# Cutting the stores of four wo gradients and the last wq gradient into row pieces in a one-core attention and MLP backward kernel

## The chip, the core and the metric

The kernel runs on one core of a Trainium2 chip. The metric is the device time of one execution in microseconds. Before the change it is 729.2 us, the median of three runs that lie between 728.81 and 729.43. The core has 16 DMA engines, and each transfer between SBUF (the core's on-chip memory, 128 partitions) and HBM is spread over some or all of them by rows of partitions.

## What is computed

The reference runs one decode step of a block and its gradients. With `xn = layernorm(x)`, the output is `x + attention(xn) + mlp(xn)`: 32 heads with a K and a V cache of 8192 x 128 each, and a gated MLP of width 1728. Returned are the output row and the gradients of x, of both caches, of wq and wo, and of the three MLP weights.

```python
q = (x @ wq).reshape(B, Sq, Hq, Dh).transpose(0, 2, 1, 3)
scores = einsum("bhqd,bhkd->bhqk", q, k) * (Dh ** -0.5)
p = softmax(scores); o = einsum("bhqk,bhkd->bhqd", p, v)
A = o.transpose(0, 2, 1, 3).reshape(B, Sq, Hq * Dh) @ wo
out = x + A + B(xn);  grads = vjp(grad_out)
```

As there is one query position, every weight gradient is an outer product of two vectors. The gradients of the caches, 32 heads x 2 x 2 MB, are outer products too, and are as large as the caches that are read.

## The kernel before

A K or V tile of one head is 128 partitions x 8192 elements, 16 KB a partition, 2 MB. Ten slots hold such tiles. A head's K and V are loaded, transposed and multiplied on PE; then the gradients are written over the tiles by DVE (line 466), and the same tiles are stored as the gradients of the caches. All of these loads and stores are issued by SP, in one order (`fifo`, line 105): a tile's store, and then the next load into a slot that has come free. SP waits in that order, for DVE before a store and for the landing of an old store before a load into its slot.

Heads are worked in groups of four (`GH`, `NG` = 8 groups). A group has a wq tile (128 partitions x 5 x 512 elements, five runs of 1 KB a partition) and a wo tile (128 partitions x 4 x 640, four runs of 1280 bytes a partition). Both are 640 KB. There are three buffers of each. Once a group's heads are done, its gradients are written over the tiles while the next group's heads run: `fin_wo` (line 518) at the first head, `fin_wq` (line 524) in five steps over the second and third. After the last step of group g, the weights of group g+3 are loaded by POOL (GpSimd) into the buffers that came free, so POOL waits at line 111 until the old gradient has landed.

The stores of these gradients go through `store_group` (line 505), which has three ways:

- groups 1 to 5, wq: rows 0 to 4 and 5 to 125 by POOL (line 508), the last two rows by SP
- all other stores of groups 0 to 6: all 128 rows in one transfer by POOL (line 512)
- group 7, both gradients: rows 0 to 67 by SP, then 68 to 72 and 73 to 127 by POOL (line 516)

Group 7's gradients are the last large work: after the outer products of head 31, `fin_od`, `fin_pe`, `fin_wo` and `fin_wq` run for it, then a short chain gives the gradient of x, and SP issues the small output rows (lines 850 and 868). The MLP with its gradients runs once, ahead of head 2; POOL stores its gradients. Each of the four engines and SP has its own instruction order; it is the order in which the program is written.

Of the kernel before, what the change touches and what calls it, by code (L numbers as in the profile page):

```python
# [16 lines left out]
P = 128  # L17
# [4 lines left out]
def kernel(  # L22
# [22 lines left out]
    nc = tc.nc  # L45
# [8 lines left out]
    GH = 4  # L54
    NG = H // GH
    GW = GH * DH
# [23 lines left out]
    dwq_v = out_4.rearrange("(ci p) n -> p ci n", p=P)  # L80
    dwo_v = out_5.rearrange("(h p) c -> p h c", p=P)
# [22 lines left out]
    def fifo(out_, in_):  # L104
        nc.sync.dma_start(out_, in_)
# [3 lines left out]
    def load_group(g, eng):  # L109
        wq_g = wpool.tile([P, NC, GW], BF16, name="wq_g", tag="wq_g")  # L110
        eng.dma_start(wq_g[:], wq_v[:, :, g * GW:(g + 1) * GW])
        wo_g = wpool.tile([P, GH, D], BF16, name="wo_g", tag="wo_g")
        eng.dma_start(wo_g[:], wo_v[:, g * GH:(g + 1) * GH, :])
        grp[g] = dict(wq=wq_g, wo=wo_g)
# [387 lines left out]
        for hh in range(GH):  # L502
            out_row(G_["od_bf"][:, hh, 0:1], G_["wo"][:, hh, :])

    def store_group(g, dst, t, split=False):
        if split:
            for lo, hi in ((0, 5), (5, 126)):
                nc.gpsimd.dma_start(dst[lo:hi], t[lo:hi])
            fifo(dst[126:P], t[126:P])
            return  # L510
        if g < NG - 1:
            nc.gpsimd.dma_start(dst, t[:])
            return
        fifo(dst[0:68], t[0:68])
        for lo, hi in ((68, 73), (73, P)):
            nc.gpsimd.dma_start(dst[lo:hi], t[lo:hi])

    def fin_wo(g):
        G_ = grp[g]
        for hh in range(GH):  # L520
            nc.vector.tensor_scalar(G_["wo"][:, hh, :], g_bc[:], G_["od"][:, hh, 0:1], None, ALU.mult)
        store_group(g, dwo_v[:, g * GH:(g + 1) * GH, :], G_["wo"])

    def fin_wq(g, ci):
        G_ = grp[g]
        wq_g, dqb = G_["wq"], G_["dqb"]
        nc.vector.scalar_tensor_tensor(wq_g[:, ci, :], wq_g[:, ci, :], 1.0, dqb, ALU.mult, ALU.mult,  # L527
                                       accum_out=dxa[:, ci, g:g + 1])
        nc.vector.tensor_scalar(wq_g[:, ci, :], dqb, xn_col[:, ci:ci + 1], None, ALU.mult)
        if ci == NC - 1:  # L530
            store_group(g, dwq_v[:, :, g * GW:(g + 1) * GW], wq_g, 1 <= g <= 5)
            grp.pop(g)
            if g + 3 < NG:
                load_group(g + 3, nc.gpsimd)
# [149 lines left out]
    def side_k(h):  # L684
        g, hh = divmod(h, GH)
        if hh == 1 and g > 0:
            fin_wq(g - 1, 0)
        elif hh == 2 and g > 0:
            fin_wq(g - 1, 3)
        elif hh == 3 and g + 1 < NG:  # L690
            prep_do(g + 1, 1)

    def side_m(h):
        g, hh = divmod(h, GH)
        if hh == 0 and g > 0:
            fin_od(g - 1)
        elif hh == 1 and g > 0:
            fin_wq(g - 1, 1)
        elif hh == 2 and g > 0:
            fin_wq(g - 1, 4)  # L700
        elif hh == 3 and g + 1 < NG:
            prep_do(g + 1, 2)
            prep_do(g + 1, 3)

    def side_v(h):
        g, hh = divmod(h, GH)
        if hh == 0 and g > 0:
            fin_wo(g - 1)
        elif hh == 1 and g > 0:
            fin_wq(g - 1, 2)  # L710
        elif hh == 2 and g + 1 < NG:
            prep_new(g + 1)
            prep_do(g + 1, 0)
        elif hh == 3 and g + 1 < NG:
            prep_cm(g + 1, hd[h]["m"][:, 324:324 + 4 * GH])
# [120 lines left out]
    fin_od(NG - 1)  # L836
    fin_pe(NG - 1)
    fin_wo(NG - 1)
    for ci in range(NC):
        fin_wq(NG - 1, ci)  # L840
# [58 lines left out]
```

## Time and profile before

| what | value |
|---|---|
| median of three runs | 729.2 us (728.81 to 729.43) |
| the profiled execution | 730.06 us |
| its span, first to last instruction | 728.3 us |
| PE, DVE, ACT, POOL busy | 600.8, 460.1, 375.7, 35.0 us |
| moved by DMA | 303.53 MB, mean 417 GB/s |
| HBM read, written | 151.34 MB, 151.34 MB |
| DMA issues of wo gradients by POOL | 7 of 640 KB, and 25 and 275 KB for the last |
| DMA issues of wq gradients by POOL | 2 of 640 KB, 5 of 605 KB, 6 of 25 KB, 1 of 275 KB |
| DMA issues of both by SP | 340 KB twice (last group), 10 KB five times |

Each time from the trace is in microseconds from the span's start. The profiled execution's own time is 1.76 us longer than its span, for what lies ahead of the first instruction and after the last. The DMA share of a stretch is the mean over the 16 engines. Queue q1 is that of SP's transfers, q0 that of POOL's, q8 and q14 fetch instructions. The trace also has a record of every packet of a DMA engine: start, duration, bytes and queue.

### The profile page before, as it was taken

How to read it: one execution, taken by the hardware profiler on the slowest of the kernel's cores; microseconds unless marked ns; L12 is line 12 of the kernel's file. 1: busy time of each engine (PE TensorE's matmuls, PEld its weight loads, DVE VectorE, ACT ScalarE, POOL GpSimd, SP SyncE). 2: the span in 40 equal slices, each digit the busy share in tenths (PEclk: the TensorE clock that was granted, in tenths of full speed). 3: DMA queues.
4: the chain of work that ended last, by engine and by line, in shares of the span. 5: the costliest groups of instructions: out<-in, count | busy, mean ns of one | idle time of the engine just before them, and what ended most of it. 6: DMA issues, size and time to landing. Idle time of an engine off the chain costs nothing.

```text
span 728.3 us, 12951 instructions
## 1 busy us (share of the span) xinstructions
PE 600.8 (82%) x5193; PEld 375.6 (52%) x5193; DVE 460.1 (63%) x811; ACT 375.7 (52%) x727; POOL 35.0 (5%) x52
## 2 busy tenths in 40 slices
PE   3989589999999999877986889878896987988840
PEld 2547456665566556544554555445563555644520
DVE  4169646677767886767556746556755665677482
ACT  3640736665666656544554546455562555645410
POOL 0010110000100000000010000000000000000000
PEclk9996799999999999999999989999998999999975
DMA  9999999999999999999999999999999999999996
GB/s 347 398 409 424 427 428 428 413 427 425 418 409 429 427 426 424 423 429 422 425 425 427 431 420 427 421 427 432 410 428 424 428 425 422 429 424 430 429 415 239
DMA packets 28358, 303.53 MB, mean 417 GB/s; under 512 B 3481, under 2 KB 5532, under 8 KB 11658
## 3 DMA queue, kind: packets, MB, share of 16 engines
q1 hardware_dynamic: 22022, 277.14, 90.4%
q0 software_dynamic: 6272, 25.56, 8.8%
q8 instruction: 41, 0.67, 0.4%
q14 instruction: 19, 0.16, 0.1%
q10 hardware_dynamic: 4, 0.00, 0.0%
HBM read 151.34 MB, written 151.34 MB: 416 GB/s over the span
## 4 chain that ended last, share of the span: by engine, by line
DMA 57%; PE 33%; DVE 5%; ACT 2%; issue 1%; SPq 0%; ACTq 0%; DVEq 0%
DMA out_dram<-kv 30%; DMA kv<-in_A_k_cache_dram 18%; PE pT L318 15%; DMA kv<-in_A_v_cache_dram 7%; PE sA L339 4%; PE X L433 3%; PE dA L339 3%; DVE kv L466 2%; PE m L356 2%; DMA wo_g<-in_A_wo_dram 2%; ACT KT L320 1%; PE gu_ps L562 1%; PE dh_ps L573 1%; DVE side L257 0%; PE pT L266 0%
## 5 line engine op out<-in xcount | busy, mean ns | idle before, releaser
L320 ACT COPY KT<-pT 128x512 f32<-128x512 f32 x512 | 287.7, 587 | 230.9 <-PE pT L318 210.3
L318 PE MATMUL pT<-ident_f,kv 128*128 128x128 f32 x2048 | 306.6, 289 | 61.6 <-DMA kv<-in_A_k_cache_dram 29.9
L318 PEld LDWEIGHTS pT<-ident_f,kv 128*128 128x128 f32 x2048 | 236.2, 148 | 155.1 <-issue 59.6
L466 DVE TENSOR_TENSOR kv<-qd,U 128x4096 bf16<-128x4096 bf16 x64 | 146.0, 2283 | 0.0
L466 DVE TENSOR_TENSOR kv<-qd,P 128x4096 bf16<-128x4096 bf16 x64 | 143.5, 2283 | 0.0
L433 PE MATMUL X<-kv,Z 128*32 128x512 bf16 x1024 | 93.5, 402 | 1.8 <-DVE Z L450 1.8
L339 PE MATMUL sA<-KT,qz 128*32 128x512 bf16 x512 | 83.9, 408 | 0.0
L339 PE MATMUL dA<-KT,qz 128*32 128x512 bf16 x512 | 83.3, 404 | 0.0
L416 DVE SCALAR_TENSOR_TENSOR U<-m,P 128x64 bf16<-128x64 f32 x32 | 7.5, 234 | 83.0 <-PE m L356 83.0
L382 DVE TENSOR_REDUCE mrow<-m 128x1 f32<-128x64 f32 x32 | 7.2, 223 | 75.1 <-PE m L356 75.0
L339 PEld LDWEIGHTS <-qz 128*32 128x32 bf16 x1024 | 29.6, 95 | 40.4 <-issue 37.7
L433 PEld LDWEIGHTS <-Z 128*32 128x32 bf16 x1024 | 32.4, 99 | 33.8 <-issue 5.7
L356 PE MATMUL m<-selc,KT 64*128 64x64 f32 x256 | 30.7, 243 | 8.6 <-ACT KT L346 8.6
L356 PEld LDWEIGHTS m<-selc,KT 64*128 64x128 f32 x256 | 21.7, 145 | 30.4 <-ACT KT L346 21.6
L376 ACT CAST qd<-pT 128x256 bf16<-128x256 f32 x32 | 11.9, 372 | 40.3 <-DVE kv L466 28.8
L389 DVE TENSOR_REDUCE negM<-m 128x1 f32<-128x128 f32 x32 | 9.3, 291 | 33.2 <-PE m L386 33.2
L527 DVE SCALAR_TENSOR_TENSOR wq_g<-wq_g,side 128x512 bf16<-128x512 bf16 x40 | 27.3, 682 | 0.0
L257 DVE SCALAR_TENSOR_TENSOR side<-wo_g,g_bc 128x640 bf16<-128x640 bf16 x32 | 26.2, 819 | 1.4 <-DMA wo_g<-in_A_wo_dram 1.1
L448 DVE SCALAR_TENSOR_TENSOR U<-m,P 128x128 bf16<-128x128 f32 x32 | 11.4, 355 | 15.8 <-PE m L446 15.8
L406 DVE RECIPROCAL rZ<-m 128x1 f32<-128x1 f32 x32 | 5.3, 166 | 24.2 <-PE m L400 24.2
L346 ACT COPY KT<-dA 64x512 f32<-64x512 f32 x32 | 18.6, 583 | 2.6 <-PE dA L339 2.6
L346 ACT COPY KT<-sA 64x512 f32<-64x512 f32 x32 | 18.6, 580 | 2.3 <-PE sA L339 2.1
(164 smaller groups left out, 377.4 us busy)
## 6 DMA issues: line engine op xcount, KB each, us to landing
out_dram<-kv SPq DMA_DIRECT2D x64, 2048.0 KB, 30.9
kv<-in_A_k_cache_dram SPq DMA_DIRECT2D x32, 2048.0 KB, 27.9
kv<-in_A_v_cache_dram SPq DMA_DIRECT2D x32, 2048.0 KB, 26.0
wq_g<-in_A_wq_dram POOLq DMA_DIRECT2D x7, 640.0 KB, 13.5
wo_g<-in_A_wo_dram POOLq DMA_DIRECT2D x7, 640.0 KB, 19.6
out_dram<-wo_g POOLq DMA_DIRECT2D x7, 640.0 KB, 15.6
kv<-in_B_w_dram SPq DMA_DIRECT2D x2, 1728.0 KB
out_dram<-kv POOLq DMA_DIRECT2D x2, 1728.0 KB, 23.2
```

The costliest lines, as they stand in the source:

```text
L257: nc.vector.scalar_tensor_tensor(junk[:], G_["wo"][:, hh, :], 1.0, g_bc[:], ALU.mult, ALU.mult, accum_out=G_["do"][:, hh:hh + 1])
L318: nc.tensor.transpose(pT[:, k * P:(k + 1) * P], W3[:, 4 * c + k, :], ident_f[:])
L320: nc.scalar.copy(KT[:].rearrange("p k w -> p (k w)"), pT[:])
L339: nc.tensor.matmul(S_[kind][q:q + QW, :], lhsT=S_["qz"][:, o:o + QW], rhs=KTb[c][:, par, :], start=(c0 == 0 and par == 0), stop=(c0 == NCH ...
L346: nc.scalar.copy(XS[0:QH].rearrange("p k w -> p (k w)"), S_.pop(kind)[0:QH, :])
L356: nc.tensor.matmul(S_["m"][:, b0:b0 + 4 * J].rearrange("p (x c k t) -> p k x c t", x=4, k=4, t=2)[:, k], lhsT=XS[0:QH, k, :], rhs=selc[0:Q ...
L376: nc.scalar.copy(qd[:].rearrange("p a d -> p (a d)"), hd[h].pop("ps_r"))
L389: nc.vector.tensor_reduce(S_["negM"][:], S_["m"][:, 2 * J:2 * J + P], AX.X, ALU.max, negate=True)
L433: nc.tensor.matmul(xg["X"][q:q + QW, :], lhsT=Z[:, o:o + QW], rhs=W[:, N4 * i:N4 * (i + 1)], start=(slot == 0 and i < 4), stop=(slot == NS ...
L448: nc.vector.scalar_tensor_tensor(S_["U2"][:], S_["V"][:, 0:J].unsqueeze(2).to_broadcast([P, J, 2]), S_["m"][:, OC + NS:OC + NS + 1], S_["P ...
L466: nc.vector.tensor_tensor(dst[:, lo * DH:hi * DH].rearrange("p (j a b) -> p j a b", a=DH // 2, b=2), vec.rearrange("p (a b) -> p a b", b=2 ...
L527: nc.vector.scalar_tensor_tensor(wq_g[:, ci, :], wq_g[:, ci, :], 1.0, dqb, ALU.mult, ALU.mult, accum_out=dxa[:, ci, g:g + 1])
```

## The change

`store_group` now takes a list of row counts, and issues one transfer for each: by POOL if the count is positive, by SP if it is negative. For most gradients the pieces are as before. What differs:

- wo of group 0 leaves as 5, 119 and 4 rows, that of group 1 as 5, 51, 4 and 68, those of groups 2 and 3 as 76, 2 and 50, all by POOL, where each was one transfer of 128 rows by POOL
- wq of group 7 leaves as 5, 51 and 72 rows by POOL, where it was 68 rows by SP and 5 and 55 by POOL

So POOL issues ten transfers more and SP one fewer. No instruction of PE, DVE or ACT changes.

```diff
-    def store_group(g, dst, t, split=False):
-        if split:
-            for lo, hi in ((0, 5), (5, 126)):
-                nc.gpsimd.dma_start(dst[lo:hi], t[lo:hi])
-            fifo(dst[126:P], t[126:P])
-            return
-        if g < NG - 1:
-            nc.gpsimd.dma_start(dst, t[:])
-            return
-        fifo(dst[0:68], t[0:68])
-        for lo, hi in ((68, 73), (73, P)):
-            nc.gpsimd.dma_start(dst[lo:hi], t[lo:hi])
+    def store_group(g, dst, t, pieces):
+        lo = 0
+        for n in pieces:
+            eng = nc.gpsimd if n > 0 else nc.sync
+            eng.dma_start(dst[lo:lo + abs(n)], t[lo:lo + abs(n)])
+            lo += abs(n)
+        assert lo == P
+
+    DWO_PIECES = {0: (5, 119, 4), 1: (5, 51, 4, 68), 2: (76, 2, 50), 3: (76, 2, 50), NG - 1: (-68, 5, 55)}
+    DWQ_PIECES = {**{i: (5, 121, -2) for i in range(1, 6)}, NG - 1: (5, 51, 72)}
...
-        store_group(g, dwo_v[:, g * GH:(g + 1) * GH, :], G_["wo"])
+        store_group(g, dwo_v[:, g * GH:(g + 1) * GH, :], G_["wo"], DWO_PIECES.get(g, (P,)))
...
-            store_group(g, dwq_v[:, :, g * GW:(g + 1) * GW], wq_g, 1 <= g <= 5)
+            store_group(g, dwq_v[:, :, g * GW:(g + 1) * GW], wq_g, DWQ_PIECES.get(g, (P,)))
```

## The prediction

> **What bounds the kernel now.** I read the DMA rows first, because a core that moves 303.53 MB in 728.3 us can hardly be bound by anything else. Columns of the queue rows: packets, MB, and the time of their packets as a share of 16 DMA engines.
>
> ```profile
> DMA  9999999999999999999999999999999999999996
> ...
> q1 hardware_dynamic: 22022, 277.14, 90.4%
> q0 software_dynamic: 6272, 25.56, 8.8%
> q8 instruction: 41, 0.67, 0.4%
> q14 instruction: 19, 0.16, 0.1%
> ```
>
> Every slice but the last is full, and the shares add up to 99.7%. The busiest compute engine, PE, has 82%. So the 16 DMA engines are the bound, and what remains to be won is at the end, where they do not stop together. The windows (length, busy times of five engines, clock, DMA share, GB/s) show that:
>
> ```profile
> 716.00:720.00 4.00, 0.37 (x1) 0.09 (x1) 0.41 (x2) 0.00 (x0) 0.00 (x0) 0.50 0.93 331
> 720.00:722.00 2.00, 0.00 (x0) 0.00 (x0) 0.00 (x0) 0.00 (x0) 0.00 (x0) 0.50 0.67 232
> 722.00:724.00 2.00, 0.00 (x0) 0.00 (x0) 0.00 (x0) 0.00 (x0) 0.00 (x0) 0.50 0.39 134
> 724.00:726.00 2.00, 0.00 (x0) 0.00 (x0) 0.00 (x0) 0.00 (x0) 0.00 (x0) 0.50 0.08 33
> 726.00:728.30 2.30, 0.00 (x0) 0.00 (x0) 0.00 (x0) 0.00 (x0) 0.00 (x0) 0.50 0.02 7
> ```
>
> No compute engine works after 720, and a share of 0.08 is little more than one engine in 16 (0.0625). One DMA engine sets the end. The final waits of SP (total us, times, longest) say for what:
>
> ```profile
> SPq L894 <- DMA out_dram<-wq_g: 5.4, 2, 4.6
> SPq L894 <- DMA out_dram<-kv: 1.6, 1, 1.6
> ```
>
> The kv store comes in last; the weight gradients are in before it. They matter because they take that engine's time, not by their own landing.
>
> **Which engine that is.** The records of single packets carry no engine number, but a packet starts 3 to 4 ns before the one ahead of it on its engine ends, so they can be chained into 16 rows. (Where two rows end in the same ns I used that a kv transfer is 8 packets of 16 KB per engine and then one of 4 bytes; ends are therefore sure as a set, and to each single row within a class only probably.) From 10 to 695 us hardly any engine is ever idle, so an engine's end is its own sum of work. The classes, in span time:
>
> - **E0 to E3** end at 721.4 to 724.5. SP's 68-row pieces at the end went to these four engines, 17 rows each. The numbers are names that I give.
> - **E4** ends at 721.8. With E0 to E3 it is in the class that got one row of each 5-row piece. Its 16 KB packets are the slowest (from 138 us on, 13.5 us in all over 611 ns each; the others 2.3 to 9.3).
> - **E5 to E15** got 11 rows of each 121-row piece (each shows thirteen packets of 4096 bytes and one of 3072, that is 55 KB; 55 packets of 3072 bytes in all is 5 groups x 11 engines), and 5 rows of each 55-row piece.
> - **E8 to E15**: eight of these eleven also carry PE's instruction fetches, strictly in turn, 5 each, and one the 41st as well. A fetch takes 0.88 to 1.15 us, and the packet behind one of them took 1.006 us in place of 0.611. The three without fetches, **E5 to E7**, end first, at 718.0 to 718.5. The other seven of the eight end at 720.7 to 724.2; the one with six fetches, which I call E8, ends at 727.0 with a 16 KB kv packet. Its sixth fetch is at 703.0.
>
> The mean end is 722.1, so perfect balance would be worth 4.9 us; the second-last engine ends 2.5 us before E8.
>
> **Where the pieces go.** 121 rows on 11 engines, 55 on 11 and 5 on 5 is "the largest divisor up to 16". The 5-row piece took the same five engines in all groups: each piece continues at the engine behind the last one's, and 5+11 comes back to E0. That the turn follows my numbering inside the eleven (E5 to E7 first, the fetch carriers after them) is assumed; no row shows it. So, rows per engine:
>
> - gradient 0 (5,119,4): E0-4 1, E5-11 17, E12-15 1
> - gradient 1 (5,51,4,68): E0-4 1, E5-7 17, E8-11 1, E12-15 17
> - gradients 2 and 3 (76,2,50), each: E0-3 19, E4-5 1, E6-15 5
> - last wq (5,51,72): E0-4 1, E5-7 17, then 72 over 12 engines: E8-15 and E0-3 6 more
>
> Against 8 rows a gradient before (4 x 8 = 32): E0-3 40, E4 4, E5 36, E6-7 44, E8-15 28. All sets but the last add up to 16, so the order holds.
>
> **The sum for E8.** (1) The wo rows: 4 fewer. A wo row is one packet of 5120 bytes, median 200 ns, shortest 196, less 3.5 overlap: 0.192 us; -0.77 us. (2) The last wq: 5 rows were 25 KB (six packets of 4096 at 159 ns and one of 1024 at 46: 0.975 us); 6 rows are seven and one of 2048 (not in the trace; between those two, I take 0.085): 1.174 us; +0.20. (3) Ten more GpSimd transfers (four become thirteen, two become three). 44 transfers left 775 packets of 4 bytes and 482 of 12 to 16, 6 to 7 ns net each: 11 ns per engine and transfer; +0.11. Sum **-0.46 us**. A row holds up no one else, so nothing more goes with it.
>
> What is late next: E6 and E7, +12 wo rows (2.3) and 17 rows of wq in place of 5 (3.31 - 0.975 = 2.3) and 0.1: 718.3 + 4.8 = 723.1. E5: 721.6. E0-3: +8 wo rows (1.5, partly in their idle time at 696 to 703), -17 rows in 1 KB packets of SP (85 x 42 ns = 3.6), +6 rows (1.2): about 0.8 earlier. E4 only gets freer (28 rows, 5.4 us). All stay over 2 us behind E8's 726.5, so the whole -0.46 counts.
>
> **What is issued, and who queues behind it.** A POOL store costs 0.6 to 0.8 us of issue:
>
> ```profile
> 462.78 0.76 POOL L512 DMA_DIRECT2D out_dram<-wo_g  x1 [9.65 <-DVE qz L363]
> 501.91 1.64 POOL L508 DMA_DIRECT2D out_dram<-wq_g  x2 [38.36 <-DVE wq_g L529]
> ...
> 708.91 1.29 POOL L516 DMA_DIRECT2D out_dram<-wo_g  x2 [37.91 <-DVE wo_g L521]
> 713.89 1.34 POOL L516 DMA_DIRECT2D out_dram<-wq_g  x2 [3.69 <-DVE dxn L845]
> ```
>
> (Start, duration, engine and line, what, and in brackets the wait before it and its releaser.) Two or three more issues (2.1 us at most) lie in the 25 to 40 us that POOL waits next for DVE; nothing is queued behind them but the wq store. Without that cover they would delay it by the same 2 us, and the loads of group g+3 with it, which are needed only a group of heads (some 85 us) later. At the end the 72-row piece is the third in POOL's queue, some 0.6 us after the old second. On E8 the first wq bytes moved at 720.5 and the last at 724.6, between kv packets that last to 727.0: 2.4 us of cover. SP loses one issue of 0.28 us; its small output stores follow sooner and land long before. Between nothing and 0.6 us of harm, I take nothing. Seventeen rows at once on an engine hold its kv packets for 3.3 us in place of 1.5; SP waits 453 us in all for kv stores and no engine ran dry over that, so I take nothing, with bounds of 1 us either way, since stalls of single packets (2 to 14 us per engine) will fall elsewhere.
>
> **A rule against it.** The Trainium skill (DMA: Bandwidth & Descriptors, "Why a DMA increments its semaphore by 16 and not by 1") states the divisor rule that the 3072-byte packets show, but also an exception for GpSimd: some copies go to all 16 engines, the row count over 16, rounded up, on each. By it E8 would have 8+9+9+9 wo rows and 9 in place of 4 of the last wq: about 1.7 us slower, as an estimate. The eleven-engine packets speak for the divisor here.
>
> **Rivals.**
>
> - *Faster: the stalls fall better* (0.22). E8's long 16 KB packets cost 7.7 us, the mean of E9-15 is 4.7; shifting the transfers' meetings may take 1 to 2.5 us of that away, until the engines at 724 bind: 729.2 - 0.5 - 1.5 = 727.2. For it: one of eight like engines is far out. Against: the three timed runs lie within 0.62 us, so the pattern repeats.
> - *Slower: the pieces start at another engine* (0.08). If the turn is not at E0 when gradient 0 leaves (a piece of 119 or 51 rows counts otherwise), or runs in another order, E8 stands where I put E0-3: 40 rows, +8 x 0.192 + 0.3 = +1.9, 731.1; where I put E6-7, +4.8, 734. It decides from about 8 extra rows on. Against: five groups landed alike.
> - *Slower: worse stalls or a late third piece* (0.05): E8's end follows the 72-row piece once that is over 2.4 us later; at 4.4 us it is 1.5 us slower, 730.7.
> - *As summed* (0.65).
>
> **Numbers.** The profiled execution took 730.06 (span 728.3), 0.86 over the median 729.2, and would go to 729.6. The difference carried to the median: 729.2 - 0.46 = **728.7**. About 0.2% (1.5 us) is what a measurement of this kernel can tell from no change. The range, 727.0 to 730.3, takes in 1.7 us of better stalls and, upward, the 1 us of harm and the 0.6 of a late third piece; about 0.1 of the chance is left out on either side, the other starting engine among it. Faster 0.22, same 0.65, slower 0.13.
>
> **What would show it.** In the packets after: 17-row runs on seven, then seven engines, 19-row runs on four; the engine with the sixth fetch still last, with a kv packet, some 0.5 us earlier; the three without fetches near 722 to 723. Wrong would be: a last packet of a wo or wq row, the last engine without instruction fetches, or DMA slices below 9 before 700.

## The result, and the profile after

The changed kernel takes **735.8 us** (median of 6 runs, 734.2 to 736.9) beside 729.3 us before (6 runs, 727.6 to 732.7). The ratio is 1.0079, with a 95% interval of 1.0052 to 1.0105: slower by 0.8%. The prediction was 728.7 us with a range of 727.0 to 730.3, so both the time and the sign are wrong. Of one of the kernels below (blocks to strided) the profiled execution was a disturbed one, so it has no row from a trace.

The profiled execution of the changed kernel took 736.89 us, its span is 735.1. The DMA part of its page:

```profile
DMA  9999999999999999999999999999999999999994
...
DMA packets 29710, 303.55 MB, mean 413 GB/s; under 512 B 5088, under 2 KB 6791, under 8 KB 13010
...
q1 hardware_dynamic: 21678, 276.79, 89.6%
q0 software_dynamic: 7968, 25.93, 9.0%
```

All slices but the last are still full, so the DMA engines are the bound as before, and no wait of a compute engine has come in. What is new is small: the mean rate is 413 in place of 417 GB/s, and q0 has 1696 packets more (7968 for 6272), most of them small (1607 more are under 512 bytes). The 344 fewer on q1 are SP's 68 rows. The ends of the engines, in the windows (length, busy times of five engines, clock, DMA share, GB/s):

```profile
720.00:722.00 2.00, 0.00 (x0) 0.00 (x0) 0.00 (x0) 0.00 (x0) 0.00 (x0) 0.50 0.94 307
722.00:724.00 2.00, 0.00 (x0) 0.00 (x0) 0.00 (x0) 0.00 (x0) 0.00 (x0) 0.50 0.66 208
724.00:726.00 2.00, 0.00 (x0) 0.00 (x0) 0.00 (x0) 0.00 (x0) 0.00 (x0) 0.50 0.42 150
726.00:728.00 2.00, 0.00 (x0) 0.00 (x0) 0.00 (x0) 0.00 (x0) 0.00 (x0) 0.50 0.30 118
728.00:730.00 2.00, 0.00 (x0) 0.00 (x0) 0.00 (x0) 0.00 (x0) 0.00 (x0) 0.50 0.19 74
730.00:732.00 2.00, 0.00 (x0) 0.00 (x0) 0.00 (x0) 0.00 (x0) 0.00 (x0) 0.50 0.09 36
```

The share that stood at 0.67 in 720 to 722 before comes two microseconds later, and the tail is longer: 0.30 is nearly five of 16 engines, where before the last window of all, from 726 on, had 0.02. So two things have happened. All engines end later, and they end further apart. By the chained packets (put into 16 rows as in the prediction) the mean end of the 16 goes from about 722.0 to about 724.9, and the last packet of data ends at 732.5 in place of 727.0. Of the 5.5 us, some 2.8 are the common delay and some 2.7 are unevenness.

What SP waits for last has changed too:

```profile
SPq L892 <- DMA out_dram<-wq_g: 13.7, 1, 13.7
```

It was the kv store before. The last data packet is now one of 1024 bytes of q0, the remainder of a 17-row run of wq (85 runs of 1 KB are 21 packets of 4096 and one of 1024). It ends a row of eleven packets of 4096 bytes one behind the other, and another 1024-byte packet, at 727.6, ends a row of 19; a six-row run has only seven, so these are two of the three engines with 17 rows.

The commonest large packet shows where the common delay comes from. A 16 KB packet of a kv tile takes 0.611 us when nothing hinders it. I add up what such packets took over that (called **stalls** below, in engine-us, the sum over 16 engines; 16 of them are 1 us of every engine). From 140 us on it was 100.7 before and is 129.7 now. By the stretch from the issue of a gradient to POOL's next store of a gradient, the four whole wo gradients had 5.2, 1.8, 3.0 and 3.0; cut, they have 19.3, 10.6, 8.0 and 6.3. The first of these numbers overstates the case: the stretch behind wo 0 is that of wq 0, which is whole in both kernels, and it fell from 16.6 to 4.6, so that the two together went only from 21.8 to 23.9. In wo 1 to 3 together the stalls rose from 7.8 to 24.9. In the profile the stalls show as a lower rate at a full share. The windows around the second wo gradient, before:

```profile
224.00:229.00 5.00, 4.92 (x49) 3.22 (x50) 3.90 (x6) 2.28 (x5) 0.37 (x1) 1.00 1.02 433
229.00:234.00 5.00, 5.00 (x41) 3.10 (x39) 4.58 (x6) 3.80 (x7) 0.00 (x0) 1.00 1.00 418
234.00:239.00 5.00, 5.00 (x49) 3.31 (x52) 3.74 (x8) 2.63 (x7) 0.00 (x0) 1.00 1.01 432
239.00:244.00 5.00, 3.67 (x48) 2.17 (x42) 3.08 (x10) 2.98 (x6) 0.00 (x0) 1.00 1.00 429
244.00:249.00 5.00, 5.00 (x42) 2.92 (x36) 5.00 (x3) 2.90 (x6) 0.00 (x0) 1.00 1.02 429
```

and after:

```profile
224.00:229.00 5.00, 5.00 (x42) 2.92 (x36) 5.00 (x3) 2.92 (x6) 0.20 (x1) 1.00 1.01 420
229.00:234.00 5.00, 5.00 (x41) 3.43 (x39) 3.36 (x11) 3.95 (x9) 0.00 (x0) 1.00 1.01 417
234.00:239.00 5.00, 3.67 (x40) 2.02 (x40) 3.56 (x7) 2.46 (x6) 0.00 (x0) 1.00 0.98 406
239.00:244.00 5.00, 5.00 (x50) 3.35 (x50) 4.48 (x6) 2.37 (x5) 0.00 (x0) 1.00 1.05 435
244.00:249.00 5.00, 5.00 (x41) 3.13 (x40) 4.01 (x6) 3.74 (x8) 0.00 (x0) 1.00 1.00 403
```

The share (last column but one) stays near 1.00, and the mean of the five rates in the last column falls from 428 to 416 GB/s. A single window proves little: that from 239 to 244 is faster than before. But over 224 to 300 us the rate is 426 before and 416 after, and of the kernels below 425 with wo cut by columns (e7) and 420 with wo cut by rows without fillers (e8). A busy DMA engine is not an engine at its rate, so the row of DMA digits cannot show this loss.

POOL's issues, as before over one line each (start, duration):

```profile
220.81 3.38 POOL L509 DMA_DIRECT2D out_dram<-wo_g  x4 [25.64 <-DVE qz L363]
...
710.70 1.29 POOL L509 DMA_DIRECT2D out_dram<-wo_g  x2 [36.76 <-DVE wo_g L519]
715.68 2.69 POOL L509 DMA_DIRECT2D out_dram<-wq_g  x3 [3.69 <-DVE dxn L843]
```

Four pieces cost POOL 3.38 us where the whole gradient cost 0.76, and it then waits for DVE all the same. The last wq is issued 1.8 us later than before (713.89), as everything in the kernel by then is.

### The profile page after: what moved, and what is told of

Same layout as the page of the kernel before. It is cut to its first block, busy times and chain, and to the rows that moved or that the text cites. A ratio compares the mean times of both kernels' runs of the same rounds, so it can differ in the third digit from the quotient of the medians.

```text
span 735.1 us, 12967 instructions
## 1 busy us (share of the span) xinstructions
PE 599.5 (82%) x5193; PEld 375.5 (51%) x5193; DVE 459.9 (63%) x811; ACT 375.8 (51%) x727; POOL 43.7 (6%) x62
## 3 DMA queue, kind: packets, MB, share of 16 engines
q0 software_dynamic: 7968, 25.93, 9.0%
## 4 chain that ended last, share of the span: by engine, by line
DMA 59%; PE 31%; DVE 5%; ACT 2%; issue 1%; SPq 0%; ACTq 0%; DVEq 0%
DMA out_dram<-kv 25%; DMA kv<-in_A_k_cache_dram 18%; PE pT L318 16%; DMA kv<-in_A_v_cache_dram 14%; PE sA L339 4%; PE dA L339 3%; PE X L433 3%; DVE kv L466 3%; PE m L356 2%; DMA wo_g<-in_A_wo_dram 2%; ACT KT L320 1%; DVE side L257 0%; PE pT L266 0%; DVE wq_g L525 0%; PE m L400 0%
## 5 line engine op out<-in xcount | busy, mean ns | idle before, releaser
L376 ACT CAST qd<-pT 128x256 bf16<-128x256 f32 x32 | 11.9, 372 | 39.6 <-DVE kv L466 28.8
L509 POOL DMA_DIRECT2D out_dram<-wq_g x15 | 12.6, 843 | 246.9 <-DVE wq_g L527 243.2
L509 POOL DMA_DIRECT2D out_dram<-wo_g x18 | 14.1, 789 | 192.1 <-DVE qz L363 155.3
## 6 DMA issues: line engine op xcount, KB each, us to landing
wq_g<-in_A_wq_dram POOLq DMA_DIRECT2D x7, 640.0 KB, 13.3
```

The lines of the kernel that those rows point to most:

```text
L376: nc.scalar.copy(qd[:].rearrange("p a d -> p (a d)"), hd[h].pop("ps_r"))
L509: eng.dma_start(dst[lo:lo + abs(n)], t[lo:lo + abs(n)])
```

## The experiments

After the result there were these theories (e1, e2 and so on are the kernels made to test them). **R**: uneven rows land on the engine that ends last. **F**: filler packets cost, the small packets that a transfer leaves on engines it does not use. **S**: the cutting itself makes kv packets stall, as **S1** by the number of GpSimd transfers, as **S2** because a row piece lets engines work on other rows than the kv tiles give them. Later came **S3** to **S5**, wordings of "any cut by rows", and **G**, in which only pieces with few or odd numbers of runs per engine cost. "E4" and the like are the prediction's names for the 16 engines. Edits are given against the piece lists of the changed kernel; "..." in a list stands for what is unchanged there, and (-68, 5, 55) is how before stores a last gradient. "Ratio" is to runs of the kernel before on the same chip.

### The two halves of the change

```diff
 e1_wo_only
+    DWQ_PIECES = {..., NG - 1: (-68, 5, 55)}
 e2_wq_only
+    DWO_PIECES = {NG - 1: (-68, 5, 55)}
```

> Only the four wo gradients are cut as in the change; the last wq gradient leaves as before (SP 68 rows, GpSimd 5 and 55). Before 729.3, with the whole change 735.8 us. Theory R (rows on the engine that ends last): E5 to E7 get 4 to 12 wo rows more, 0.8 to 2.3 us, and lose nothing else, so 731.6. Theory F (filler: the engines that a GpSimd transfer leaves out get 4-byte descriptors in its place, and packets stall around such transfers, on all engines): with the whole change 1.03 MB less had been moved by 700 us, 2.4 us at 420 GB/s, and that is all from the wo cuts, so the mean end of the 16 engines moves by 2.4 and the time goes to 731.7 to 733; the DMA records show it before 700 us.

> Only the last wq gradient is cut as in the change (5, 51, 72 rows by GpSimd); the four wo gradients are whole. Theory R: E5 to E7 get 17 rows in place of 5, 2.3 us; if one of them is the engine that ends last, 731.6, if not, 727 + at most 0.2 on the others, so 729.5. Theory F: the loss of 2.4 us before 700 us is gone; what is left is the uneven end, 729.3 to 732. A third theory (the last gradient reaches the engines later by GpSimd than by SP) gives 731 to 732 with a wq packet as the last one.

The wo pieces alone have a ratio of 1.0050 (1.0035 to 1.0065, 732.8 us), the wq pieces alone 1.0023 (1.0006 to 1.0040, 730.9 us). Together they make about the whole, so these are two costs that add up. The stalls belong to the first: 48.0 engine-us in the stretches of the four wo gradients with wo cut, 15.2 with wo whole. In the second the last data packet is one of 1024 bytes of q0, the 17-row run of the last wq, as in the full change.

### Even pieces, and long pieces in turn

```diff
 e3_even_pieces
+    DWO_PIECES = {0: (48, 64, 16), 1: (16, 48, 16, 48), 2: (64, 16, 48), 3: (64, 16, 48), NG - 1: (-68, 5, 55)}
+    DWQ_PIECES = {..., NG - 1: (16, 48, 64)}
 e5_alternate
+    DWO_PIECES = {0: (119, 9), 1: (9, 119), 2: (119, 9), 3: (9, 119), NG - 1: (-68, 5, 55)}
+    DWQ_PIECES = {..., NG - 1: (-68, 5, 55)}
```

> As many GpSimd transfers as in the change, but each piece is a multiple of 16 rows (wo 48,64,16; 16,48,16,48; 64,16,48 twice; last wq 16,48,64), so that every engine gets the same rows and no filler is needed. Theory R: the engines that end last get 3 rows more in the last wq (0.6 us), 729.9. Theory F: no filler, no loss, 729.3 to 730. If the number of transfers or GpSimd's issue were the cause, 735 as with the change.

> The four wo gradients leave as 119 and 9 rows, and 9 and 119, in turn: one half of the engines gets 17 rows each and the other 1, then the other way round; over the four, E0-6 and E9-15 get 36 rows, E7-8 4, in place of 32. The last wq as before. Theory R: 4 rows more on the last engine, 0.8 us, 730.1. Theory F: filler of 17 or 18 packets per engine and gradient as in gradient 0 of the change, whose 30 us showed 14 engine-us more of long 16 KB packets than before (0.9 us per engine), so four times 0.9 and 0.8 for the rows: 732 to 734.

e3: 1.0058 (1.0042 to 1.0075, 733.8 us). e5: 1.0067 (1.0045 to 1.0089, 734.2 us). e3 takes R and F away as main causes: in the wo gradients every engine gets the same rows as before, in the last wq the engines that end last get 3 rows more (0.6 us), there is not one filler more (416 packets of 16 bytes, 457 before), and it is nearly as slow as the change. Its stalls are 56.8 engine-us in the four stretches, those of e5 48.0.

### Columns for rows, and the last wq

```diff
 e7_columns_wo: wo 0 to 3 in (1, 2, 1), (1, 1, 1, 1), (2, 1, 1), (2, 1, 1) heads of all rows
+            nc.gpsimd.dma_start(dwo_v[:, g * GH + h0:g * GH + h0 + n, :], G_["wo"][:, h0:h0 + n, :])
 e8_even_rows_wo: wo as in e3, the last wq as before
 e4_wq_pool_old_places: wo as before
+    DWQ_PIECES = {..., NG - 1: (5, 55, 68)}
 e9_whole_wq: wo as before
+    DWQ_PIECES = {NG - 1: (-68, 5, 55)}
```

> wo of groups 0 to 3 leaves in 3, 4, 3 and 3 transfers as in the change, but cut by heads, so that each transfer has all 128 rows, 8 on every DMA engine; the last wq as before. Theory S1 (each further GpSimd transfer makes kv packets stall, whatever its rows): about as slow as the change in wo alone, 3 to 4 us over before, and 6 to 24 engine-us of stalls per wo gradient. Theory S2 (what stalls is that a cut brings rows to other engines than a whole transfer does): within 0.7 us of before, 2 to 7 engine-us of stalls. Theory F (only fillers, the packets of 4 bytes for engines that a transfer does not use, cost): as before, too.

> wo of groups 0 to 3 leaves in row pieces that are all multiples of 16, in the change's numbers of transfers; every engine gets its 8 rows a gradient as before and no filler is written; the last wq as before. S1 and S2: 3 to 5 us slower than before, with 8 to 24 engine-us of stalls per gradient. F and R (uneven rows on the engine that ends last): within 0.7 us of before, and then the slowness of the earlier even kernel would be its last wq piece of 64 rows by POOL.

> only the last wq differs from before: 5, 55 and 68 rows, all by POOL, the 68 rows in place of SP's transfer and on the same four engines. The change's last wq alone cost 1.7 us. If that came from moving rows to the engines that end last (R): within 0.7 us of before. If it came from SP's transfer now being one of POOL's, issued third and with fillers on twelve engines (F): 1.5 us or more over before, and SP's last long wait is for the wq gradient.

> undoes the cut of the wq gradients 1 to 5 too (each one transfer of 128 rows by POOL); wo and the last wq as before. Theory S (cutting a gradient that GpSimd stores makes kv packets stall): stalls of 36 to 60 engine-us go, 2 to 4 us of the mean end; but engine E4, which then carries 8 rows of each of the five in place of 1, gains 5 x 7 x 0.195 = 6.8 us and would end near 728 less the 2 to 4: 725 to 728, so 1 to 2 us faster or the same. If stalls do not follow the cuts: E4 ends last at 728.6 and the time is 1 to 2 us over before.

**e7** against **e8** is the sharpest pair of the study. Both make 3, 4, 3 and 3 transfers, both give every engine an equal share of bytes. By columns the ratio is 0.9995 (0.9983 to 1.0007) with 11.9 engine-us of stalls, by rows 1.0055 (1.0033 to 1.0076) with 48.9. So S1 falls for three or four transfers: cutting costs nothing, cutting by rows does.

**e4** came out between its two theories: 1.0015 (1.0002 to 1.0027), 0.9 us in the medians. It does not tell how much of e2's cost is SP's transfer being POOL's and how much is its place.

**e9** undoes the row cut that the kernel before already had, that of five wq gradients. Their stalls go from 47.3 to 20.8 engine-us, so they followed the cuts there too. Its ratio is 1.0024 (1.0012 to 1.0036), which is the time that was expected if stalls did not follow the cuts: one engine is late and sets the end. By its rows it is E4, though no packet names it. Its windows show it alone:

```profile
724.00:726.00 2.00, 0.00 (x0) 0.00 (x0) 0.00 (x0) 0.00 (x0) 0.00 (x0) 0.50 0.06 25
726.00:728.00 2.00, 0.00 (x0) 0.00 (x0) 0.00 (x0) 0.00 (x0) 0.00 (x0) 0.50 0.08 33
```

The others are done by 724.0, 3 us sooner than before; the last data packet ends at 729.07. With its 35 rows more (0.195 us each) and nothing else changed E4 would end at 721.8 + 6.8 = 728.6. So the late engine got none of the 2 to 4 us that fewer stalls were expected to give it, and why is open.

### Whose rows they are

```diff
 e10_strided_rows (e11, e12, e13: the one, the other or both of the two slices as 16 * j:16 * j + 16)
+        if g < 4:
+            for j in range(8):
+                nc.gpsimd.dma_start(dwo_v[j::8, g * GH:(g + 1) * GH, :], G_["wo"][j::8])
+            return
```

> wo of groups 0 to 3 leaves in 8 transfers each, of 16 rows that stand 8 apart (rows j, j+8, j+16 and so on). Every engine gets one row a transfer, and if a whole transfer gives engine e the rows 8e to 8e+7, then each engine still gets its own rows. Theory S2 (stalls come when engines work on rows that are not their own): within 0.8 us of before and 2 to 7 engine-us of stalls per gradient, although there are 28 transfers more. Theory S3 (stalls come with every cut by rows): 3 to 6 us slower, 8 to 25 engine-us per gradient.

> the same 8 transfers of 16 rows, but of neighbouring rows (16j to 16j+15), so that all 16 engines work in the rows of two of them. S2 and S3 both: 3 to 6 us slower than before, 8 to 25 engine-us of stalls per gradient. If it is as fast as before, both fall.

> SBUF rows in blocks of 16 neighbours, written to HBM rows that stand 8 apart; the rows of wo's gradients 0 to 3 come out in another order than the reference's. If S2 is a matter of the SBUF side: as slow as the blocks, 3 to 6 us over before. If of the HBM side: as before, within 0.8 us.

> SBUF rows that stand 8 apart, written to blocks of 16 neighbouring HBM rows; again the rows of wo's gradients 0 to 3 come out in another order. If S2 is a matter of the SBUF side: as before, within 0.8 us. If of the HBM side: 3 to 6 us slower.

The last two leave the rows of these gradients in another order than the reference, so they serve for the time alone. All four are slower than before: e10 1.0029 (1.0016 to 1.0043), e11 1.0053 (1.0035 to 1.0072), e12 1.0046 (1.0031 to 1.0061), e13 1.0038 (1.0023 to 1.0053). Stalls in the wo stretches are 44.0, 41.2 and 33.6 for e10, e11 and e13. S2 expected e10 to be as fast as before, and it is not; this counts against S2 if a whole transfer does give each engine eight neighbouring rows, as the expectation assumes. The four intervals overlap at their edges, so that SBUF and HBM side cannot be told apart and no difference between them is claimed.

### Number, turn, and eight rows

```diff
 e17_eight_columns: wo 0 to 3 in 8 transfers of half a head, 128 rows each
+                nc.gpsimd.dma_start(dwo_v[:, g * GH + h, lo:lo + 320], G_["wo"][:, h, lo:lo + 320])
 e14_turned_whole
+    DWO_PIECES = {0: (100, 28), NG - 1: (-68, 5, 55)}
+    DWQ_PIECES = {6: (100, 28), NG - 1: (-68, 5, 55)}
 e16_fifteen_engines: wo as before
+    DWQ_PIECES = {1: (4, 1, 120, -3), 2: (1, 120, -7), 3: (1, 120, -7), 4: (1, 120, -7), 5: (1, 121, -6), NG - 1: (-68, 5, 55)}
```

> wo of groups 0 to 3 leaves in 8 transfers each, cut by columns (half a head, 640 bytes of each of the 128 rows). As many transfers as the two kernels of 8 row pieces. Theory S1 (number of transfers, felt only with many): 2 to 4 us slower than before, 5 to 15 engine-us of stalls per gradient. Theory S4 (row pieces, which leave the engines with other amounts or at other times than the whole does): within 0.8 us, 2 to 7 engine-us.

> all wq and wo gradients of groups 0 to 6 whole, but for wo 0 and wq 6, which leave as 100 and 28 rows: 10 engines and then 14, so that from wo 0 on every transfer of GpSimd begins eight engines later, and from wq 6 on as before. Beside the kernel with whole wq gradients. Theory S2 (rows on other engines than the kv tiles have them on): stalls of 5 to 15 engine-us after each of the 11 whole gradients between, where that kernel has 2 to 5, and 4 to 6 us slower than it, 735 or more. S4: as that kernel in between (2 to 5 engine-us each), 731 to 732.5.

> wo and last wq as before. The wq gradients 1 to 5 leave as 1 and 120 rows by GpSimd and 7 by SP (the first with 4 rows ahead and 3 by SP, the last as 1, 121 and 6): the 120 rows go to 15 engines, 8 each, and pass over E4. Beside the kernel with whole wq gradients, E4 carries 7 rows less of each. S4 in its milder form (8 rows on every engine that takes part is as good as whole): stalls per wq of 3 to 6 engine-us, E4 ends 6.8 us earlier than with whole gradients and the last engine at about 725: 726 to 728 us, faster than before. S2, or any cut by rows: stalls of 8 to 14 per gradient and 729 to 731.

**e17** has 8 transfers a gradient as e10 has, and costs nothing: 0.9999 (0.9982 to 1.0017), 21.9 engine-us. The POOL rows show that it is not a matter of POOL's time either, as the faster of the two issues longer. e17:

```profile
222.52 4.48 POOL L523 DMA_DIRECT2D out_dram<-wo_g  x8 [23.93 <-DVE wo_g L519]
```

e10:

```profile
220.85 4.05 POOL L522 DMA_DIRECT2D out_dram<-wo_g  x8 [25.84 <-DVE qz L363]
```

S1 is done with. **e14** was to turn all transfers between wo 0 and wq 6 by eight engines, and the whole gradients between stall as in e9: 20.9 engine-us for wq 1 to 5 (e9 20.8) and 1.5, 2.5 and 2.2 for wo 1 to 3. More stalls come with its two cut gradients: wo 0 has 18.7 (4.8 in e9; with wq 0 24.7 for 18.6), wq 6 9.2 (2.7 in e9), and the last two have 13.1 (4.0 in e9). If the whole transfers did turn, rows on other engines cost nothing and S2 falls. That they turned is assumed from the pieces: no packet shows which rows of a whole transfer an engine has. So S2 has e10 and e14 against it, each under an assumption that was not tested. The ratio, 1.0036 (1.0021 to 1.0052), is 0.0012 over that of e9, and the two intervals overlap.

**e16** missed. A piece of one row does not go to one engine: its window holds five packets of 1024 bytes, so the row's five runs were spread over five engines. The turn therefore moved on by four engines with each gradient, and another engine than E4 was passed over. The time, 1.0072 (1.0047 to 1.0097), says nothing on the theory. The stalls do: 27.6 engine-us for five gradients that have 8 rows on each of 15 engines and a few single rows, against 47.3 with 11-row pieces and 20.8 whole.

### The mildest row cut, and a version that beats both

```diff
 e20_two_halves: the last wq as before
+    DWO_PIECES = {0: (64, 64), 1: (64, 64), 2: (64, 64), 3: (64, 64), NG - 1: (-68, 5, 55)}
 e21_four_quarters: the last wq as before
+    DWO_PIECES = {0: (32,) * 4, 1: (32,) * 4, 2: (32,) * 4, 3: (32,) * 4, NG - 1: (-68, 5, 55)}
 e19_three_cut: wo as before
+    DWQ_PIECES = {**{i: (5, 121, -2) for i in (1, 3, 5)}, NG - 1: (-68, 5, 55)}
```

> wo of groups 0 to 3 leaves in two row pieces of 64, 4 rows on every engine; the rest as before. Theory S5 (any transfer that gives an engine other than its full 8 rows leads to stalls): 2 to 5 us slower than before, 6 to 20 engine-us of stalls per gradient. Theory G (only pieces whose runs per engine are few or no multiple of 8; here 4 rows are 16 runs): within 0.8 us, 2 to 7 engine-us.

> the same in four pieces of 32 rows, 2 rows and 8 runs on every engine. S5: 2 to 5 us slower. G: within 0.8 us.

> wo and the last wq as before, wq of groups 1, 3 and 5 cut as before, wq of groups 2 and 4 whole. Linear between the kernel before (five cuts: E4 ends at 721.8, the last of the others at 727.0) and the one with whole wq gradients (none: 731.5 and 724.0): E4 at 725.7, the others at 725.8, so the last data packet some 1.2 us earlier than before and 727.5 to 728.3 where before has 729. If the stalls do not follow the cuts one by one, 729 to 730.

Two halves: 1.0043 (1.0028 to 1.0058), 37.6 engine-us. Four quarters: 1.0038 (1.0022 to 1.0054), 43.0. Theory G falls; S5 stands, in this wording: a GpSimd store that gives its engines other than eight rows each is followed by stalls. It is not the only source of them: the whole wq 0 has 8.9 to 19.3 engine-us in the kernels whose wo 0 is whole or in columns.

**e19** takes two of the five old cuts back, and is **faster than both kernels**: 727.4 us (726.5 to 730.1), ratio 0.9980 (0.9968 to 0.9993). Its windows, to hold beside those of before in the prediction:

```profile
720.00:722.00 2.00, 0.00 (x0) 0.00 (x0) 0.00 (x0) 0.00 (x0) 0.00 (x0) 0.50 0.52 194
722.00:724.00 2.00, 0.00 (x0) 0.00 (x0) 0.00 (x0) 0.00 (x0) 0.00 (x0) 0.50 0.25 101
724.00:726.00 2.00, 0.00 (x0) 0.00 (x0) 0.00 (x0) 0.00 (x0) 0.00 (x0) 0.50 0.02 8
```

0.67, 0.39 and 0.08 before: engines end earlier, and the last data packet is in at 724.9, 2.1 us sooner. It gains by fewer row cuts, where the change made more of them. The three cut wq gradients have 7.5, 6.3 and 8.4 engine-us, the two whole ones 3.8 and 4.0. The expectation, 1.2 us sooner, was not right in its working: it took 731.5 for the end of E4 in e9, whose last data packet ended at 729.07.

### All stalls side by side

| wo 0 to 3 leave as | kernels | stalls in the wo 0 to 3 stretches, engine-us |
|---|---|---|
| whole | before, e2, e4, e9, e16, e19 | 13.0, 15.2, 13.4, 10.8, 17.7, 10.2 |
| columns of all rows | e7, e17 | 11.9, 21.9 |
| rows, uneven | after, e1, e5 | 44.2, 48.0, 48.0 |
| rows, even | e3, e8, e10, e11, e13, e20, e21 | 56.8, 48.9, 44.0, 41.2, 33.6, 37.6, 43.0 |

(e14 cuts one of the four and is left out.) Each number is of one trace. Still the two groups stand apart, at most 21.9 against at least 33.6. Much of that distance is wo 0, where stalls in part only come earlier: wo 0 and the whole wq 0 behind it have together 12.7 to 29.4 when wo 0 is whole or in columns, and 22.5 to 28.7 when it is cut by rows. Without wo 0 the groups stand apart less, at most 11.8 (e17) against at least 15.4 (e20). Over everything from 140 us on, and for kernels with the wq of before cut as before, it is 85.5 to 100.7 (before, e2, e4, e7, e17; mean 92.4) against 114.0 to 148.1 (after, e1, e3, e5, e8, e10, e11, e13, e20, e21; mean 130.8). The difference of the means, 38 engine-us, is 2.4 us of every engine, and the kernels with only wo cut by rows are 2.3 to 5.3 us over before in the medians. In the eleven traced kernels that differ in wo alone, before among them, the span of the profiled execution rises with these stalls (correlation 0.92), by 0.10 us for each engine-us, where 1/16 would be 0.06. By this estimate the 16 KB packets account for about six tenths of the loss; the rest was not traced to anything.

## Why the prediction was wrong, point by point

- **The bound: right.** DMA is full to the tail, and no compute engine or queue came in between.
- **Where the pieces go: right.** The numbers of packets are those of the divisors: twelve of 2048 bytes for 72 rows (six rows on each of twelve engines; there were none before), and runs of 17 rows on seven, then seven engines and of 19 rows on four. The rule of the other sort, rows over 16 rounded up, was not seen in any of the piece sizes used here.
- **The step that failed: stalls.** "Seventeen rows at once on an engine hold its kv packets for 3.3 us in place of 1.5; ... so I take nothing, with bounds of 1 us either way, since stalls of single packets will fall elsewhere", and "A row holds up no one else, so nothing more goes with it". Stalls did not fall elsewhere, they grew: from 140 us on 29 engine-us more, 1.8 us of each engine. Cutting by rows alone, with even rows, no fillers and an unchanged end, cost 3.1 and 4.0 us (e20 and e8, 0.0043 and 0.0055 of 729). What the runs show in its place: kv packets on all engines are held up when wo is cut by rows (e8), and not when it is cut by columns (e7). The trace of before held a hint, if not a clean one: its five cut wq gradients had 6.8 to 13.3 engine-us each, its whole gradients from wo 1 on 1.8 to 3.4, but the whole wq 0 had 16.6. I had looked at the stalls by engine, not by what was being stored at the time.
- **"+0.11 for ten more transfers": mis-sized.** I took the small packets of q0 as a fixed number per engine and transfer. They are not, see below: 1439 more packets of 16 bytes at 10.8 ns, 7.3 net of the overlap, are 10.5 engine-us, 0.66 us of each engine on the mean. It is the smaller part; e8 and e20 have none of them and are slow.
- **"E5 to E7", the engines said to end first: wrong.** That these three are the ones without fetches was said to be assumed. In e2 they get 17 rows of the last wq and their old rows of wo, so they should end near 718.3 + 2.3 = 720.6, all three. The long rows of 4096-byte packets show two of them ending at 722.7 and 726.6. So at least two of the three were late already, and they are the ones that got most rows (36 and 44 of wo in place of 32, and 17 of wq in place of 5). In the changed kernel two of them end at 727.6 and 732.5 in place of 721.6 and 723.1, and the second is the last of all. In the chained packets of after I read PE's fetches on three of E8 to E11, three of E12 to E15, on E5, and on one of E6 and E7, which would be the reason; chains can change places where two packets end together, so this reading is argued and not shown. From the 720.7 to 727.0 of the engines with fetches my own +4.8 would have given 725.5 to 731.8 in place of 723.1. The sum of -0.46, made for an engine with fewer rows, was then not the sum of the engine that ends last. Which of the two 44-row engines was last cannot be told, so the split of the 2.7 us of unevenness is argued too; that the last wq alone costs (e2, 1.0023) and ends in such a run fits it.
- **The issue side: right for wo.** POOL's longer issues lie in its waits for DVE, and e17 shows that 4.48 us of issue cost nothing. For the last wq, where nothing was taken, e4, where the same rows go by POOL in place of SP, measured 0.9 us.
- **The rivals.** "Slower: worse stalls or a late third piece" at 0.05 named one thing that happened, the stalls, but for one engine and with a price of 730.7; the last packet was of the second piece of wq, not of the third. "The pieces start at another engine" at 0.08 came nearest: its "runs in another order", with the late engine where E6 and E7 were put, had a price of 734, and with 1.8 us of stalls that is 735.8. That this equals the measured time is partly luck, since the fillers' 0.66 us are not in it. The price of the stalls could have been worked out from the trace of before: its five cut wq gradients have 9.5 engine-us on the mean, the seven whole gradients from wo 1 on 2.6, so four more cuts are 4 x 6.8 = 27 engine-us or 1.7 us of each engine. That alone would have put the forecast at 730.4, on the other side. What "would be wrong" was listed rightly: a last packet of a wq row was there.

The Trainium skill (DMA: Bandwidth & Descriptors, "Rules for kernel authors") advises against two transfers to disjoint halves of the partitions, since they share the same engines anyway, and for one transfer of all 128. The runs agree and add a price: two halves for four gradients of 640 KB made the kernel 0.43% slower, while three to eight pieces by columns cost nothing that could be measured.

**What stays open** is why row pieces do this. It is not their number (e17), not fillers or uneven rows (e8, e20), and not the length of POOL's issue; the place of the rows has e10 and e14 against it, under the assumptions named there. Whether the same cuts issued by SP would cost as much was not run. The stalls come in bursts in which many engines have packets of 0.8 to 1.4 us at the same time, and partly when the pieces are gone: in e10 the pieces of wo 1 moved between 224 and 237 us, and the largest burst, 5.4 engine-us, lies between 241 and 244. The stretches of wq 1 to 5, with the wq of before, tend to be worse too behind wo gradients cut by rows: 44.9 to 72.9 engine-us in ten kernels, 31.0 to 47.3 in five with wo whole or in columns, so the two overlap. That points to something lasting, such as engines that have got out of step over the kv tiles, but a measure of that was not found in the packets, and it is not shown.

## What to carry to other kernels

When the DMA engines are full, read the duration of the commonest large packet against what is stored at that time: the share of busy time does not show stalls, the rate and the packet do. A large store by GpSimd is best left whole or cut by columns of all 128 partitions; a cut by rows, to shift a few rows from one engine to others, is paid for by all 16 engines (here 2.3 to 4.4 us in the medians, with four gradients cut evenly), and is worth it only while one engine is later than the others by more than that. Before rows are given to engines that "end first", show by their packets which ones these are, best with a kernel that gives a few rows to those engines alone.

## What the runs showed of the hardware that was not expected

- **Fillers.** A GpSimd transfer that goes to fewer than 16 engines leaves small packets on the others: as many descriptors of 4 bytes as each of the used engines has runs, four to a packet of 16 bytes. Of 120 rows on 15 engines (40 runs each) the window holds 10 packets of 16 bytes; of 100 and 28 rows on 10 and 14 engines 64 (6 x 10 + 2 x 2). Each takes 10.8 ns, but also a turn between two kv packets: the 17 fillers for a run of 17 rows take some 9 to 10 us, about one in the time of each kv packet (0.611 us). A gradient in four pieces moved over 225 to 254 us, where the whole one took 228 to 234.
- **Stalls after row pieces**: 114 to 148 engine-us from 140 us on, where whole gradients and columns have 85 to 101 (all with wq 1 to 5 cut as before). In wo 1 to 3 alone it is 15 to 33 for 6 to 12.
- **A one-row piece** of five runs went to five engines.
- **PE's instruction fetches** are 41 packets on q8 of 0.88 to 1.17 us each, among packets of 0.611. By my reading of the chains they go to 8 of the 16 engines in turn, and these eight are not neighbours in the order in which pieces are dealt out; the ends in e2 fit that, but no row shows it.
